# Quad 0 of a ReLU-squared attention: k split between a plain and a casting transfer, and turned ahead of q

## The chip, the cores and the metric

The kernel runs on one core of one Trainium2 chip. The metric is the device time of one execution in microseconds (us); lower is better. The engines are named as the profile names them: PE is TensorE's matmul, PEld its weight load, DVE is VectorE, ACT is ScalarE, POOL is GpSimd, SP is SyncE. SP, ACT and POOL can issue transfers (DMA); those that SP and ACT issue here are plain copies of float32, those of POOL cast float32 to bf16 on the way.

## The reference

Attention with a squared ReLU in place of softmax, and then a two-layer network with a leaky activation whose slope differs by column. Cut to what is computed:

```python
batch, n_heads, seq, head_dim = (8, 12, 448, 64)
n_tokens, d_model, d_ff = (3584, 768, 2048)

def _attn_ref(q, k, v):
    S = q.shape[2]
    scale = 1.0 / np.sqrt(q.shape[-1])
    scores = scale * np.matmul(q, k.transpose(0, 1, 3, 2))
    attn = np.maximum(scores, 0.0) ** 2 / S
    return np.matmul(attn, v)

def _moe_ref(x, w_in, w_out, alpha):
    h = x @ w_in
    g = np.maximum(h, 0.0) + alpha * np.minimum(h, 0.0)
    return g @ w_out
```

The heads of a token are put side by side between the two: `x` has 8 x 448 rows and 12 x 64 columns. All inputs and the output are float32.

## The kernel before

The attention is worked in 24 quads: quad `n` is four heads of one batch entry (three quads to an entry). A quad's q, k and v lie in tiles of 128 partitions x 2 x 7 x 64: two heads on the two halves of the partitions, two more in the second dimension, and the 448 rows of a head as 64 partitions x 7 blocks. Block `j` is thus 64 rows of each head.

For every quad, q and k have to be turned, so that the 64 features stand on the partitions: `T` is 128 x 2 x 7 x 128, with index 0 of its second dimension for q and 1 for k. Quads 0 to 5 are turned on TensorE (`turn_pe`): 14 transposes each for q and k into a PSUM bank, and a copy from there to `T`. Later quads are turned by a transposing transfer that SP issues (`turn_dma`, lines 159 to 166).

Then, for each of seven blocks `j`, `score_mm` (lines 171 to 180) makes the scores of k's block `j` against all of q with four matmuls in a pair of PSUM banks. It needs all seven blocks of q in `T` and one block of k. `relu` (line 182) takes the pair to a bf16 tile `rl`, on ScalarE ("A", line 185) or VectorE ("D", line 187) as a letter says; for the first quads the letters are `ADAAAAA`, so score 1 goes to VectorE. `square` (line 190) squares it into `at`, mostly on VectorE (line 195). `attnv` (line 198) multiplies all seven `at` tiles of a quad with v (line 205) and scales the result into `xT`. `sc` makes scores and relus of a list of blocks, `sq` the squares that are still owed.

The two layers follow: `f1` (lines 237 to 255) makes one of 16 slices of the hidden layer for one batch entry, six matmuls (line 239) and the activation on ScalarE and VectorE; `f2` (lines 257 to 270) makes the output of 128 rows by 384 columns from 16 matmuls (line 262) and sends it out.

All of this is one program in the order in which it is written; each engine runs its own instructions in that order, and waits between engines follow from the tiles that they share. PSUM's eight banks are handed out by hand: `take_pair` and `take_bank` give the pair or the bank that was taken longest ago, `hold` keeps one.

The start of the program is what the change touches. Lines 120 to 124: SP issues all of q of quad 0 as float32 (`qfirst`, 448 KB) and then alpha, ACT issues all of k (`kfirst`, 448 KB). GpSimd makes the identity matrix (line 125), then issues v of quad 0 (line 126), and q, k, v of quads 1 and 2 (lines 136 to 138), each as a casting transfer; the first half of `w_in` follows (lines 278 and 279). TensorE runs 36 matmuls of the identity with itself (lines 127 to 129). Lines 130 to 135 cast quad 0 to bf16: q's blocks 0 to 3 on VectorE and 4 to 6 on ScalarE, then k's blocks 0 and 1, and 2 to 6, on ScalarE. Line 280 turns quad 0, q first: each part of the copies goes into its own bank, and all four copies to `T` are VectorE's:

```python
    load_w_in(0)
    load_w_in(1)
    turn_pe(0, ((0, 4, "D"), (4, NJ, "D")), ((0, 2, "D"), (2, NJ, "D")))
    sc(ch(0, 0, 4))
    sq(3)
    load_qk(3)
    sc(ch(0, 4, 6))
    turn_pe(1)
    sc(ch(0, 6, 7))
    sq(4)
```

The next quads come in the same manner: quad 1 is turned after score 5 of quad 0, `attnv(0)` stands behind the first three scores of quad 1, quad 2 is turned behind score 3 of quad 1.

Of the kernel before, what the change touches and what calls it, by code (L numbers as in the profile page):

```python
# [10 lines left out]
F32 = mybir.dt.float32  # L11
BF16 = mybir.dt.bfloat16
# [4 lines left out]
NJ = 7  # L17
# [3 lines left out]
def kernel(  # L21
# [10 lines left out]
    nc = tc.nc  # L32
    B, H, S, D = q.shape
    d_model, d_ff = moe_w_in.shape
    assert H * D == d_model and S == PP * NJ and D == 64 and H % 4 == 0 and B % 2 == 0
    NG = H // 4
# [7 lines left out]
    singles = ctx.enter_context(tc.tile_pool(name="singles", bufs=1))  # L44
    raw_pool = ctx.enter_context(tc.tile_pool(name="raw", bufs=3))
    v_pool = ctx.enter_context(tc.tile_pool(name="v", bufs=7))
    perm_pool = ctx.enter_context(tc.tile_pool(name="perm", bufs=2))
    T_pool = ctx.enter_context(tc.tile_pool(name="T", bufs=4))
# [8 lines left out]
    ident = singles.tile([128, 128], BF16)  # L57
# [4 lines left out]
    psum = ps_pool.tile([128, 8, 512], F32)  # L62
# [5 lines left out]
    def take(lo, n):  # L68
        clock[0] += 1
        for i in range(lo, lo + n):  # L70
            taken[i] = clock[0]
# [12 lines left out]
    def take_bank():  # L84
        i = min(range(8), key=lambda i: (taken[i], i))
        take(i, 1)
        return psum[:, i]


    raw, vraw = {}, {}  # L90

    def load_qk(n):
        b, g = divmod(n, NG)
        for name, src in (("q", q), ("k", k)):
            t = raw_pool.tile([128, 2, NJ, D], BF16, tag=name, name=f"{name}raw")
            flat = src[b].rearrange("(m two) (pp j) d -> (two pp) m (j d)", two=2, j=NJ)
            nc.gpsimd.dma_start(out=t.rearrange("p m j d -> p m (j d)"), in_=flat[:, 2 * g:2 * g + 2])  # L97
            raw[(n, name)] = t

    def load_v(n):  # L100
        b, g = divmod(n, NG)
        t = v_pool.tile([128, 2, NJ, D], BF16, tag="v", name="vraw")
        flat = v[b].rearrange("(m two) (pp j) d -> (two pp) m (j d)", two=2, j=NJ)
        nc.gpsimd.dma_start(out=t.rearrange("p m j d -> p m (j d)"), in_=flat[:, 2 * g:2 * g + 2])  # L104
        vraw[n] = t
# [4 lines left out]
    def load_w_in(i):  # L110
        lo, hi = 512 * i, 512 * i + 512
        for hf in range(2):
            for e in range(2):
                nc.gpsimd.dma_start(out=w_in_sb[64 * hf:64 * hf + 64, :, e, lo:hi],  # L114
                                    in_=w_in_v[hf, e, :, :, lo:hi])
# [1 line left out]
    def load_w_out(h):  # L117
        nc.gpsimd.dma_start(out=w_out_sb[:, h], in_=w_out_v[h])

    first = {}  # L120
    for name, src, eng in (("q", q, nc.sync), ("k", k, nc.scalar)):
        first[name] = singles.tile([128, 2, NJ * D], F32, name=f"{name}first")
        eng.dma_start(out=first[name], in_=src[0].rearrange("(m two) (pp j) d -> (two pp) m (j d)", two=2, j=NJ)[:, :2])
    nc.sync.dma_start(out=alpha_sb, in_=moe_alpha.rearrange("(kf p) -> p kf", p=128))
    make_identity(nc, ident)
    load_v(0)
    warm = psum[:, 7, :128]
    for _ in range(36):
        nc.tensor.matmul(warm, ident, ident, start=True, stop=True)
    for name, cut in (("q", ((0, 4, nc.vector.tensor_copy), (4, NJ, nc.scalar.copy))),  # L130
                      ("k", ((0, 2, nc.scalar.copy), (2, NJ, nc.scalar.copy)))):
        t = raw_pool.tile([128, 2, NJ, D], BF16, tag=name, name=f"{name}raw")
        for lo, hi, copy in cut:
            copy(t[:, :, lo:hi].rearrange("p m j d -> p m (j d)"), first[name][:, :, D * lo:D * hi])  # L134
        raw[(0, name)] = t
    for n in range(1, NG):
        load_qk(n)
        load_v(n)


    T = {}

    def turn_pe(n, cuts=((0, NJ, "D"),), cuts_k=((0, NJ, "D"),)):
        t = T_pool.tile([128, 2, NJ, 128], BF16, tag="T", name="T")
        for i, name in enumerate("qk"):
            src = raw.pop((n, name))
            for lo, hi, eng in (cuts, cuts_k)[i]:
                ps = take_bank().bitcast(BF16)
                for j in range(lo, hi):
                    for s in range(2):  # L150
                        nc.tensor.transpose(ps[64 * s:64 * s + 64, 128 * j:128 * j + 128], src[:, s, j], ident)  # L151
                dst = t[:, i, lo:hi].rearrange("p j c -> p (j c)")
                if eng == "D":
                    nc.vector.tensor_copy(dst, ps[:, 128 * lo:128 * hi])  # L154
                else:
                    nc.scalar.copy(dst, ps[:, 128 * lo:128 * hi])
        T[n] = t

    def turn_dma(n):
        p = perm_pool.tile([128, 2, NJ, 2, D], BF16, tag="perm", name="perm")  # L160
# [10 lines left out]
    def score_mm(n, j):  # L171
        ps = take_pair()
        t = T[n]
        for r in range(2):
            for c in range(2):
                nc.tensor.matmul(ps[64 * c:64 * c + 64, r, :S],  # L176
                                 t[64 * r:64 * r + 64, 1, j, 64 * c:64 * c + 64],
                                 t[64 * r:64 * r + 64, 0, :, 64 * c:64 * c + 64],
                                 start=True, stop=True)
        return ps  # L180

    def relu(ps, eng):
        rl = rl_pool.tile([128, 2, S], BF16, tag="rl", name="rl")
        if eng == "A":
            nc.scalar.activation(rl, ps[:, :, :S], ACTF.Relu)  # L185
        else:
            nc.vector.tensor_scalar(rl, ps[:, :, :S], 0.0, None, ALU.max)  # L187
        return rl
# [31 lines left out]
    def sc(chunks):  # L220

        for n, j, eng in chunks:
            late.append((n, j, relu(score_mm(n, j), eng)))

    def sq(k=99, eng="D"):
        for g in late[:k]:
            square(*g, eng)
        del late[:k]
# [8 lines left out]
    def f1_mm(ps, b, ff, ks):  # L237
        for km in ks:
            nc.tensor.matmul(ps, w_in_sb[:, km // 2, km % 2, bass.ts(ff, 128)],  # L239
                             xT[b][:, km // 2, km % 2, :],  # L240
                             start=(km == 0), stop=(km == KM - 1))

    def f1_out(ps, b, ff):
        if b // 2 not in gT:
            gT[b // 2] = g_pool.tile([128, KF, 2 * S], BF16, tag="g", name="gT")
        neg = neg_pool.tile([128, S], F32, tag="neg", name="neg")
        nc.scalar.activation(neg, ps, ACTF.Relu, scale=-1.0)  # L247
        nc.vector.scalar_tensor_tensor(gT[b // 2][:, ff, (b % 2) * S:(b % 2) * S + S],  # L248
                                       neg, beta_sb[:, ff:ff + 1], ps, ALU.mult, ALU.add)
        sq(1)  # L250
# [24 lines left out]
    def ch(n, lo, hi, p=pat):  # L275
        return [(n, j, p[j]) for j in range(lo, hi)]

    load_w_in(0)
    load_w_in(1)
    turn_pe(0, ((0, 4, "D"), (4, NJ, "D")), ((0, 2, "D"), (2, NJ, "D")))  # L280
    sc(ch(0, 0, 4))
    sq(3)
    load_qk(3)
    sc(ch(0, 4, 6))
# [3 lines that stand above are left out]
# [5 lines left out]
    sq(2)  # L293
    sc(ch(1, 3, 4))
    turn_pe(2)
    sq(1)
    sc([(1, 4, "D"), (1, 5, "A"), (1, 6, "A")])
# [57 lines left out]
    f1s(0, 8, 9)  # L355
    ps = take_bank()[:, :S]
    f1_mm(ps, 0, 9, range(KM))
    turn_pe(4, ((0, NJ, "A"),))
    f1_out(ps, 0, 9)
    load_qk(7)  # L360
    load_v(7)
# [40 lines left out]
    for ff in range(4):  # L402
        ps = take_bank()[:, :S]
# [92 lines left out]
```

## Time and profile before

| what | value |
|---|---|
| time, median of 9 runs | 389.15 us (388.89 to 392.31) |
| the profiled execution's own time | 389.23 us |
| its span, first to last instruction | 387.5 us |
| PE busy | 378.6 us (98%), 3228 matmuls |
| DVE busy | 265.9 us (69%), 420 instructions |
| ACT busy | 206.5 us (53%), 332 instructions |
| POOL busy | 63.2 us (16%) |
| mean granted clock of TensorE | 0.998 |
| matmuls of line 239 | 768, 149.5 us |
| matmuls of line 262 | 912, 151.1 us |
| matmuls of line 176 (scores) | 672, 45.7 us |
| matmuls of line 205 (attention times v) | 672, 37.0 us |
| transfers, whole span | 43.06 MB, 111 GB/s |
| transfers, first 30 us | 5.72 MB, 191 GB/s |

The profile is of one execution. A busy PE need not be a PE at its peak, because matmuls are pipelined and their ends are modelled. Times in the views count from the start of the span; the 1.7 us between span and time lie outside of it. An instruction's row gives its start, the time that it (or a group of its like) takes, its engine, its line, and what it writes and reads; brackets give the idle time of the engine before it and what ended that.

### The profile page before, as it was taken

How to read it: one execution, taken by the hardware profiler on the slowest of the kernel's cores; microseconds unless marked ns; L12 is line 12 of the kernel's file. 1: busy time of each engine (PE TensorE's matmuls, PEld its weight loads, DVE VectorE, ACT ScalarE, POOL GpSimd, SP SyncE). 2: the span in 40 equal slices, each digit the busy share in tenths (PEclk: the TensorE clock that was granted, in tenths of full speed). 3: DMA queues.
4: the chain of work that ended last, by engine and by line, in shares of the span. 5: the costliest groups of instructions: out<-in, count | busy, mean ns of one | idle time of the engine just before them, and what ended most of it. 6: DMA issues, size and time to landing. Idle time of an engine off the chain costs nothing.

```text
span 387.5 us, 7916 instructions
## 1 busy us (share of the span) xinstructions
PE 378.6 (98%) x3228; PEld 211.9 (55%) x3228; DVE 265.9 (69%) x420; ACT 206.5 (53%) x332; POOL 63.2 (16%) x94
## 2 busy tenths in 40 slices
PE   8799999999999999999999999999999999999995
PEld 6444564555665456645555455654555545655564
DVE  3977876777868878789655896689754887626300
ACT  4977686355555664455445554547543475434311
POOL 7467211512022202022110221020000000000000
PEclk9999999999999999999999999999999999999999
DMA  9999999999493775787292871936024200120023
GB/s 181 186 204 205 203 213 214 147 164 201 102 156 69 117 131 73 130 139 114 46 176 51 136 120 42 179 57 133 22 63 108 70 0 23 42 61 2 20 71 75
DMA packets 71093, 43.06 MB, mean 111 GB/s; under 512 B 38160, under 2 KB 71056, under 8 KB 71056
## 3 DMA queue, kind: packets, MB, share of 16 engines
q0 software_dynamic: 26496, 22.35, 39.6%
q1 hardware_dynamic: 44128, 19.65, 24.3%
q10 hardware_dynamic: 432, 0.56, 0.4%
q8 instruction: 25, 0.41, 0.4%
q14 instruction: 12, 0.10, 0.1%
HBM read 45.62 MB, written 11.01 MB: 146 GB/s over the span
## 4 chain that ended last, share of the span: by engine, by line
PE 94%; ACT 1%; DVE 1%; DMA 1%; issue 0%; ACTq 0%
PE psum L239 38%; PE psum L262 38%; PE psum L176 9%; PE psum L205 8%; ACT rl L185 1%; PE psum L151 1%; DMA qfirst<-in_q_dram 1%; DVE at L195 1%; DVE T L154 0%; DVE rl L187 0%; ACT osb L264 0%; ACTq L270 0%; DVE qraw L134 0%; ACTq L264 0%; ACT xT L215 0%
## 5 line engine op out<-in xcount | busy, mean ns | idle before, releaser
L262 PE MATMUL psum<-w_out_sb,gT 128*128 128x384 bf16 (+2 forms) x912 | 151.1, 323 | 0.0
L239 PE MATMUL psum<-xT,w_in_sb 128*128 128x448 bf16 x768 | 149.5, 353 | 0.4 <-ACT rl L185 0.4
L262 PEld LDWEIGHTS <-gT 128*128 128x128 bf16 x912 | 86.7, 98 | 63.0 <-issue 8.2
L239 PEld LDWEIGHTS <-w_in_sb 128*128 128x128 bf16 x768 | 73.7, 98 | 72.4 <-issue 5.7
L248 DVE SCALAR_TENSOR_TENSOR gT<-neg,beta_sb,psum 128x448 bf16<-128x448 f32 x128 | 83.1, 676 | 30.7 <-ACT neg L247 30.7
L247 ACT ACTIVATE neg<-psum 128x448 f32<-128x448 f32 x128 | 69.3, 547 | 64.0 <-PE psum L239 60.2
L185 ACT ACTIVATE rl<-psum 128x896 bf16<-128x896 f32 x112 | 97.3, 935 | 1.1 <-PE psum L176 1.1
L195 DVE TENSOR_TENSOR at<-rl 128x896 bf16<-128x896 bf16 x162 | 90.7, 616 | 0.0
L187 DVE TENSOR_SCALAR rl<-psum 128x896 bf16<-128x896 f32 x56 | 60.8, 1086 | 41.0 <-PE psum L176 41.0
L264 ACT COPY osb<-psum 128x384 f32<-128x384 f32 (+2 forms) x57 | 27.0, 474 | 105.6 <-PE psum L262 96.6
L176 PE MATMUL psum<-T 64*64 64x448 bf16 x672 | 45.7, 356 | 2.5 <-DVE T L154 0.9
L97 POOL DMA_DIRECT2D qraw<-in_q_dram x23 | 16.5, 718 | 171.4 <-DVE perm L162 166.6
L205 PE MATMUL psum<-at,vraw 64*64 64x448 bf16 x672 | 37.0, 351 | 0.5 <-ACT rl L185 0.2
L205 PEld LDWEIGHTS <-vraw 64*64 64x64 bf16 x672 | 24.2, 106 | 10.8 <-issue 2.5
L176 PEld LDWEIGHTS <-T 64*64 64x64 bf16 x672 | 18.1, 105 | 21.6 <-issue 15.0
L216 DVE TENSOR_SCALAR xT<-psum 128x448 bf16<-128x448 f32 x23 | 14.4, 624 | 16.2 <-PE psum L205 11.8
L97 POOL DMA_DIRECT2D kraw<-in_k_dram x23 | 16.5, 717 | 14.9 <-PE psum L239 7.0
L104 POOL DMA_DIRECT2D vraw<-in_v_dram x24 | 17.3, 722 | 1.2 <-issue 0.6
L215 ACT ACTIVATE xT<-psum 128x448 bf16<-128x448 f32 x23 | 12.7, 553 | 3.0 <-PE psum L205 3.0
L162 DVE COPY perm<-qraw 128x896 bf16<-128x896 bf16 x18 | 11.0, 611 | 4.2 <-DMA T<-perm 2.6
L114 POOL DMA_DIRECT2D w_in_sb<-in_moe_w_in_dram x16 | 10.1, 629 | 8.1 <-DMA kraw<-in_k_dram 2.8
L162 DVE COPY perm<-kraw 128x896 bf16<-128x896 bf16 x18 | 10.9, 607 | 0.0
(22 smaller groups left out, 42.3 us busy)
## 6 DMA issues: line engine op xcount, KB each, us to landing
out_dram<-osb SPq DMA_DIRECT2D x110, 96.0 KB, 2.2
vraw<-in_v_dram POOLq DMA_DIRECT2D x24, 224.0 KB, 7.5
qraw<-in_q_dram POOLq DMA_DIRECT2D x23, 224.0 KB, 4.7
kraw<-in_k_dram POOLq DMA_DIRECT2D x23, 224.0 KB, 6.7
w_in_sb<-in_moe_w_in_dram POOLq DMA_DIRECT2D x16, 192.0 KB, 8.0
w_out_sb<-in_moe_w_out_dram POOLq DMA_DIRECT2D x2, 1536.0 KB, 18.5
kfirst<-in_k_dram ACTq DMA_DIRECT2D x1, 448.0 KB, 4.6
qfirst<-in_q_dram SPq DMA_DIRECT2D x1, 448.0 KB, 4.3
```

Source lines behind the costliest of these rows:

```text
L97: nc.gpsimd.dma_start(out=t.rearrange("p m j d -> p m (j d)"), in_=flat[:, 2 * g:2 * g + 2])
L162: nc.vector.tensor_copy(p[:, i], raw.pop((n, name)).rearrange("p s j d -> p j s d"))
L176: nc.tensor.matmul(ps[64 * c:64 * c + 64, r, :S], t[64 * r:64 * r + 64, 1, j, 64 * c:64 * c + 64], t[64 * r:64 * r + 64, 0, :, 64 * c:64 * ...
L185: nc.scalar.activation(rl, ps[:, :, :S], ACTF.Relu)
L187: nc.vector.tensor_scalar(rl, ps[:, :, :S], 0.0, None, ALU.max)
L195: nc.vector.tensor_tensor(a, rl, rl, ALU.mult)
L205: nc.tensor.matmul(ps[64 * s:64 * s + 64, r, :S], vv[64 * r:64 * r + 64, s, j, :], a[64 * r:64 * r + 64, s], start=(j == 0), stop=(j == NJ ...
L239: nc.tensor.matmul(ps, w_in_sb[:, km // 2, km % 2, bass.ts(ff, 128)], xT[b][:, km // 2, km % 2, :], start=(km == 0), stop=(km == KM - 1))
L247: nc.scalar.activation(neg, ps, ACTF.Relu, scale=-1.0)
L248: nc.vector.scalar_tensor_tensor(gT[b // 2][:, ff, (b % 2) * S:(b % 2) * S + S], neg, beta_sb[:, ff:ff + 1], ps, ALU.mult, ALU.add)
L262: nc.tensor.matmul(ps, gT[sb][:, ff, bass.ts(c, 128)], w_out_sb[:, hf, ff, lo:hi], start=(ff == 0), stop=(ff == KF - 1))
L264: nc.scalar.copy(o[:, lo:hi], ps)
```

## The change

Quad 0's k is split. Its first four blocks of seven (`FIRST = 4`) still come by ACT's plain transfer, now 256 KB, and are cast by ScalarE in one copy. The other three come as GpSimd's first casting transfer, straight into the bf16 tile. q still comes whole by SP's plain transfer; its two casts stay on VectorE and ScalarE, but ScalarE casts k's four blocks before q's last three.

GpSimd's order changes: the rest of k comes first, then q and k of quad 1, v of quad 0, q and k of quad 2, v of quad 1, v of quad 2 (before: v of quad 0, then q, k, v of quad 1, then q, k, v of quad 2).

The identity is multiplied 30 times instead of 36. `turn_pe` takes a list of parts, so that q and k can be turned piece by piece in any order. For quad 0 it turns k's blocks 0 to 3 first, with ScalarE's copy into `T`, then q's two parts with VectorE's copies; then come scores 0 to 2; then k's blocks 4 to 6 are turned, with VectorE's copy, and score 3 follows. Quad 4's call is written in the new form with the same engines as before (q's copy on ScalarE, k's on VectorE).

```diff
+    FIRST = 4
+    first, flat0 = {}, {}
+    for name, src, eng, hi in (("q", q, nc.sync, NJ), ("k", k, nc.scalar, FIRST)):
+        first[name] = singles.tile([128, 2, hi * D], F32, name=f"{name}first")
+        flat0[name] = src[0].rearrange("(m two) (pp j) d -> (two pp) m (j d)", two=2, j=NJ)[:, :2]
+        eng.dma_start(out=first[name], in_=flat0[name][:, :, :hi * D])
+        raw[(0, name)] = raw_pool.tile([128, 2, NJ, D], BF16, tag=name, name=f"{name}raw")
     nc.sync.dma_start(out=alpha_sb, in_=moe_alpha.rearrange("(kf p) -> p kf", p=128))
     make_identity(nc, ident)
+    nc.gpsimd.dma_start(out=raw[(0, "k")][:, :, FIRST:].rearrange("p m j d -> p m (j d)"),
+                        in_=flat0["k"][:, :, FIRST * D:])
+    warm = psum[:, 7, :128]
+    for _ in range(30):
+        nc.tensor.matmul(warm, ident, ident, start=True, stop=True)
+    for name, lo, hi, copy in (("k", 0, FIRST, nc.scalar.copy), ("q", 0, 4, nc.vector.tensor_copy),
+                               ("q", 4, NJ, nc.scalar.copy)):
+        copy(raw[(0, name)][:, :, lo:hi].rearrange("p m j d -> p m (j d)"), first[name][:, :, D * lo:D * hi])
+    load_qk(1)
     load_v(0)
-    warm = psum[:, 7, :128]
-    for _ in range(36):
-        nc.tensor.matmul(warm, ident, ident, start=True, stop=True)
-    for name, cut in (("q", ((0, 4, nc.vector.tensor_copy), (4, NJ, nc.scalar.copy))),
-                      ("k", ((0, 2, nc.scalar.copy), (2, NJ, nc.scalar.copy)))):
...
-    for n in range(1, NG):
-        load_qk(n)
-        load_v(n)
+    load_qk(2)
+    load_v(1)
+    load_v(2)
...
+    def turn_pe(n, parts=(("q", 0, NJ, "D"), ("k", 0, NJ, "D"))):
+        if n not in T:
+            T[n] = T_pool.tile([128, 2, NJ, 128], BF16, tag="T", name="T")
+        for name, lo, hi, eng in parts:
+            ps = take_bank().bitcast(BF16)
+            for j in range(lo, hi):
+                for s in range(2):
+                    nc.tensor.transpose(ps[64 * s:64 * s + 64, 128 * j:128 * j + 128], raw[(n, name)][:, s, j], ident)
+            dst = T[n][:, "qk".index(name), lo:hi].rearrange("p j c -> p (j c)")
+            copy = nc.vector.tensor_copy if eng == "D" else nc.scalar.copy
+            copy(dst, ps[:, 128 * lo:128 * hi])
...
-    turn_pe(0, ((0, 4, "D"), (4, NJ, "D")), ((0, 2, "D"), (2, NJ, "D")))
-    sc(ch(0, 0, 4))
+    turn_pe(0, (("k", 0, FIRST, "A"), ("q", 0, 4, "D"), ("q", 4, NJ, "D")))
+    sc(ch(0, 0, 3))
+    turn_pe(0, (("k", FIRST, NJ, "D"),))
+    sc(ch(0, 3, 4))
...
-    turn_pe(4, ((0, NJ, "A"),))
+    turn_pe(4, (("q", 0, NJ, "A"), ("k", 0, NJ, "D")))
```

More of the change, by code (lines that the diff above doesn't have):

```diff
@@ L118, in load_w_out @@
         nc.gpsimd.dma_start(out=w_out_sb[:, h], in_=w_out_v[h])
[L120 to L123, printed above, removed]
+    FIRST = 4
[5 more added lines that the diff above has]
+        raw[(0, name)] = raw_pool.tile([128, 2, NJ, D], BF16, tag=name, name=f"{name}raw")
@@ L124 @@
     nc.sync.dma_start(out=alpha_sb, in_=moe_alpha.rearrange("(kf p) -> p kf", p=128))
     make_identity(nc, ident)
-    load_v(0)
-    warm = psum[:, 7, :128]
-    for _ in range(36):
-        nc.tensor.matmul(warm, ident, ident, start=True, stop=True)
-    for name, cut in (("q", ((0, 4, nc.vector.tensor_copy), (4, NJ, nc.scalar.copy))),
-                      ("k", ((0, 2, nc.scalar.copy), (2, NJ, nc.scalar.copy)))):
[L132 to L135, printed above, removed]
@@ L136 @@
-    for n in range(1, NG):
-        load_qk(n)
-        load_v(n)
-    T = {}
[L143 to L157, printed above, removed]
+    nc.gpsimd.dma_start(out=raw[(0, "k")][:, :, FIRST:].rearrange("p m j d -> p m (j d)"),
+                        in_=flat0["k"][:, :, FIRST * D:])
```

## The prediction

> **What bounds the kernel now.** I read the busy time by stretch first, to find where anything but TensorE sets the pace (columns: stretch, length, then PE, PEld, DVE, ACT, POOL busy, clock, DMA share, GB/s).
>
> ```profile
> 7.60:14.80 7.20, 5.79 (x114) 3.43 (x112) 7.18 (x13) 7.20 (x10) 3.15 (x5) 1.00 1.22 190
> 14.80:19.70 4.90, 3.63 (x64) 1.83 (x61) 4.86 (x10) 4.90 (x8) 2.92 (x5) 1.00 1.18 185
> 19.70:22.00 2.30, 1.57 (x21) 0.71 (x20) 2.30 (x6) 2.30 (x5) 1.62 (x3) 1.00 1.23 205
> 22.00:30.00 8.00, 8.00 (x85) 4.35 (x85) 5.51 (x9) 4.80 (x8) 5.16 (x9) 1.00 1.25 203
> ```
>
> Until 22 us ScalarE and VectorE are both full while PE has gaps; from 22 us PE is full. So work added to ScalarE or VectorE before 22 us, or a later start of their packed stretch, delays the end by as much. Then the chain of waits over the first 30 us (start, us, what), for what starts that stretch:
>
> ```profile
> 0.74 4.25 DMA qfirst<-in_q_dram
> ...
> 5.02 0.44 DVE qraw L134
> ...
> 5.50 1.75 PE psum L151 x27
> ...
> 7.27 0.50 DVE T L154
> ...
> 7.82 0.60 PE psum L176 x8
> 8.42 0.60 ACT rl L185
> ```
>
> The landing of q, a cast, the transposes, a copy of T and the scores stand in a row. The timeline of 0 to 8 us (start, us, instruction) gives the durations:
>
> ```profile
> 1.36 4.02 PE L129 MATMUL psum<-ident 128*128 128x128 bf16 x36 [1.36 <-POOL ident masks.py:199]
> ...
> 5.50 0.96 PE L151 MATMUL psum<-ident,qraw 128*64 128x128 bf16 x14
> ...
> 6.18 0.89 DVE L154 COPY T<-psum 128x512 bf16<-128x512 bf16 x3 [0.74 <-PE psum L151]
> 6.25 0.98 PE L151 MATMUL psum<-ident,kraw 128*64 128x128 bf16 x14
> ...
> 7.16 1.04 PE L176 MATMUL psum<-T 64*64 64x448 bf16 x12
> 7.27 0.49 DVE L154 COPY T<-psum 128x640 bf16<-128x640 bf16 x1 [0.20 <-PE psum L151]
> ```
>
> VectorE's first relu starts at 7.79 and its first square at 8.79; ScalarE's first relu starts at 7.59 and lasts 0.92. Last, the DMA queues from 2.75 to 4.50 us (q10 carries k, q1 carries q):
>
> ```profile
> q10 hardware_dynamic: 187, 0.34, 50.4%
> q1 hardware_dynamic: 186, 0.33, 48.7%
> ```
>
> The two queues take turns packet by packet. In the microsecond before, q1 had sent 70 packets and q10 one, so q has a head start.
>
> **The change, part by part.**
>
> *Landings.* Before, q lands at 0.74+4.25 = 4.99 and k at 0.74+4.6 = 5.34. k's 256 packets shrink from 1792 to 1024 bytes. The stretch in which both take turns moves 186x(1792+1024) = 0.52 MB instead of 0.67 MB, at the window's 380 GB/s 0.37 us less; k's remaining 68 packets save 0.14 us more. So q lands at 4.62 and k at 4.83: k still last, although it now goes first. Bounds for k: 4.65 if the queues shared bytes rather than packets (2x262 KB at 380 GB/s from 2.75, and the 0.52 from data to landing), 5.34 if a packet cost the same whatever its size. I take packets by bytes, since 380 GB/s held at one packet size.
>
> *k's cast on ScalarE, ahead of q.* ScalarE's casts of 384 and 640 columns took 0.51 and 0.72, so 512 take 0.61: 4.86 to 5.47. PE starts transposing at 5.52 (a cast's end to PE's start was 0.05), where it started at 5.50. q's casts finish beside that: VectorE 0.43 from 4.65, ScalarE 0.51 from 5.47.
>
> *Transposes before the first score: 22 instead of 18.* 28 starts took 1.45 us (5.50 to 6.95), 0.054 each, with 0.31 for the last to end. The q blocks that VectorE copies first are now the 9th to 16th: ready at 5.52+15x0.054+0.31 = 6.64 (before 6.16). Its copies of 0.425 and 0.348 overlap by 0.08 and end at 7.35; the first score followed the copies by 0.09, so 7.44 instead of 7.16: **0.28 later**. The k copy that moves to ScalarE is ready at 6.21; by ScalarE's 0.91 for 896 columns and 0.55 for 448 it takes 0.55 to 0.6 and is done by 6.83, hidden under VectorE's q copies by 0.5; without that cover its excess would add whole.
>
> *k's last three blocks.* Their 0.35 copy stands behind the relu of score 1 on VectorE, inside the packed stretch; the 0.28+0.49 of k copies that it had before lay ahead of that stretch. Score 1 ends 0.61 after the first score's start (eight score matmuls took 0.57 at 7.82), so the relu starts at 8.05 instead of 7.79, its follower 1.00 later, and the squares another 0.27 after that: 9.32 instead of 8.79, **0.53 late**. Score 3 waits for that copy (end 9.40): its relu starts at 9.40+0.05+0.38 = 9.83 where three relus in a row put it at 7.59+2x0.92 = 9.43, 0.40 late. Queued behind the copy on VectorE are all squares and the T copies of quad 1; ScalarE gets 0.1 us of idle. What is late next is attnv(0) and then quad 2's transposes, both inside the packed stretch.
>
> *The casting transfer.* It stands where v of quad 0 stood, which was issued at 1.44 and landed 6.0 later, at 7.44. It moves 96 of 224 KB; the casting queue moved 0.40 MB from 5.25 to 7.5 us, 178 GB/s, so 128 KB less is 0.72 less: landing between 6.7 and 7.44. PE reaches these blocks after score 2, near 8.1, and VectorE wants them at 9.05; a landing after 8.7 would hold PE and every score behind it, one for one. The cover is 1.2 to 2 us; cost 0. The Trainium skill, "DMA: Bandwidth & Descriptors", Specifications, says that pieces under 512 bytes are written by read-modify-write, and these are 384; no row here shows one, and by it the landing would go toward the late end, still covered: the sum is the same.
>
> *Order on GpSimd's queue.* v(0) becomes fourth, where the fourth landed at 10.9 and its reader starts at 12.0; v(1) seventh (15.4, needed at 17.8); v(2) eighth (16.35, needed at 23.56). q and k of quad 1 move up by 0 to 0.72; those of quad 2 keep their places. w_in has 96 KB more ahead of it, 0.54 at most, against 1.3 of slack (its first four pieces land by 20.2, first read 21.46). Cost 0. Alpha's transfer stays behind q on its queue. Line 358's call for quad 4, rewritten, does what it did: 0.
>
> *30 warming matmuls instead of 36.* 36 took 4.02 us, 0.106 a start; 30 end at 4.74. Then PE idles 0.78 us until 5.52, where it idled 0.12, and again from about 6.9 to 7.44, where it transposed. The granted clock reads 1.00 in every stretch, yet the 14 transposes of q took 0.96 at 5.50 and 0.58 at 9.37, and weight loads of k 0.165 against 0.109: PE ran at half pace until about 7.16, 5.8 us after its first matmul. The bounds: paced by time since the first work, fast from 7.16, cost 0 (no gain: it isn't earlier); paced by unbroken work, fast from 5.52+5.8 = 11.3, or from 7.44+5.8 = 13.2. If PE is slow through score 3 only, scores take 0.37 each instead of 0.19: the relu of score 1 starts at 8.39, squares at 9.66, 0.87 late, and score 3's relu at about 10.36, 0.93 late.
>
> The Trainium skill, "TensorE: Matmul & The Clock Gate", Part 1, says that the clock is released by a sustained busy window of some 3.4 us that runs freely of the kernel. By it 30 matmuls (3.38 us) no longer fill one, and full pace would come between 8.9 and 14: 0.9 to 1.8 late in all, an estimate from that page; this trace's 5.8 us neither proves nor denies it.
>
> *Sum.* Against this execution's own 389.23 (span 387.5 and 1.7 around it, 0.08 above the median of 389.15): +0.53 with the pace as before, +0.93 with a pace late by some 3 us. I take the middle, +0.75: 389.23+0.75 = 389.98, say 390.0.
>
> **The rivals.**
>
> *The pace comes after 11 us: slower.* Quad 1's 28 transposes begin near 10.9; slow, their first copy starts at 11.72 (pace at 11.3: seven slow, seven fast, 0.22) to 11.97 (never fast), the k copy at 12.7 instead of 10.9. That is 1.3 to 1.8 late, **390.8**. For it: the 0.78 gap and the shorter warming. Against: PE still works most of the time from 1.36. It decides once pace comes later than about 11.0, where quad 1's copies pass 10.39+1.17.
>
> *k early, or the delay absorbed: no change.* With k at 4.65 all is 0.18 less; with quad 1's q and k landing earlier some of the wait at the T copies may go: **389.3**. Against: VectorE and ScalarE show no idle to absorb anything.
>
> *A late landing: slower.* k at 5.34 adds 0.51 to either sum (390.3 to 390.7), or the casting transfer lands past 8.7+0.7: **390.5**. For it: smaller packets. Against: the covers above.
>
> *A real gain: faster.* The first relus would have to start 1.2 us earlier, with k and q both down near 3.5: **387.9**. For it: 192 KB less ahead of the first cast. Against: the rate of the DMA queues allows 0.5.
>
> **How the numbers follow.** A measurement of this kernel can tell about 0.3% from no change, 1.17 us: slower is above 390.3, faster below 388.0. Forecast 0.41 (389.6 to 390.2, no change), late pace 0.36 (slower), absorbed 0.11 (no change), late landing 0.05 (slower), gain 0.07. So faster 0.07, same 0.52, slower 0.41. Range 389.0 to 391.2: from the absorbed case less a spread of 0.3 to the late pace with its 1.8 and 0.2.
>
> **What would show it.** Right: k lands after q, near 4.8; first score near 7.4; VectorE's k copy directly behind its first relu, squares from 9.3 on or later; the transposes of quad 1 show the pace (0.58 or 0.96 for 14). Wrong if k lands before 4.4, if score 3's relu starts before 9.4, or if PE after 22 us is no longer without gaps.

## The result, and the profile after

The changed kernel took 389.77 us (median of 25 executions, 388.90 to 390.61); the kernel before, over 76 executions, 389.06 (388.88 to 392.31). The ratio is 1.0017, with a 95% interval from 1.0011 to 1.0023: slower by a little, and inside the 0.3% that was called no change. The median moved by 0.71 us where 0.75 was forecast. The median hides how it came about: of the 25 times, 8 lie at 388.9 to 389.1, 8 at 389.5 to 390.1 and 9 at 390.4 to 390.6. The kernel before has 74 of its 76 times within 388.9 and 389.4.

The profiled execution of the changed kernel is one of the first group: 389.00 us, span 387.2. Its busy time by stretch, with the columns as before:

```profile
7.60:14.80 7.20, 5.67 (x114) 3.29 (x108) 7.06 (x13) 7.20 (x10) 3.45 (x6) 1.00 1.24 196
14.80:19.70 4.90, 3.73 (x72) 2.04 (x67) 4.79 (x9) 4.90 (x8) 3.15 (x5) 1.00 1.16 181
19.70:22.00 2.30, 1.67 (x25) 0.72 (x21) 2.30 (x6) 2.30 (x5) 1.45 (x3) 1.00 1.26 210
22.00:30.00 8.00, 8.00 (x85) 4.28 (x85) 5.58 (x10) 4.75 (x8) 5.22 (x8) 1.00 1.24 202
```

The shape is that of before: ScalarE is full up to 22 us, VectorE all but 0.14 and 0.11 us, PE full behind it. The timeline of the first 10 us:

```profile
1.36 3.38 PE L133 MATMUL psum<-ident 128*128 128x128 bf16 x30 [1.36 <-POOL ident masks.py:199]
...
4.77 0.61 DVE L136 CAST qraw<-qfirst 128x512 bf16<-128x512 f32 x1 [4.77 <-DMA qfirst<-in_q_dram]
5.03 0.62 ACT L136 CAST kraw<-kfirst 128x512 bf16<-128x512 f32 x1 [2.47 <-DMA kfirst<-in_k_dram]
...
5.70 0.41 PE L153 MATMUL psum<-ident,kraw 128*64 128x128 bf16 x8 [0.96 <-ACT kraw L136]
5.95 0.56 PE L153 MATMUL psum<-ident,qraw 128*64 128x128 bf16 x14
...
7.12 0.76 PE L175 MATMUL psum<-T 64*64 64x448 bf16 x12 [0.62 <-DVE T L156]
...
8.52 0.38 PE L175 MATMUL psum<-T 64*64 64x448 bf16 x4 [0.35 <-ACT rl L184]
8.75 0.34 DVE L156 COPY T<-psum 128x384 bf16<-128x384 bf16 x1
...
9.15 0.57 PE L175 MATMUL psum<-T 64*64 64x448 bf16 x8 [0.25 <-DVE T L156]
```

k lands at 5.00 (0.74 + 4.26), behind q at 4.77, and the order of the steps is the predicted one. But 14 transposes take 0.56 us already at 5.95, where the kernel before needed 0.96 at 5.50: in this execution PE had its full pace before its first transpose, and the first score stands at 7.12 in spite of 22 transposes ahead of it. The second profile of the same kernel, of an execution of 391.61 us, shows the other kind:

```profile
6.17 0.96 PE L153 MATMUL psum<-ident,qraw 128*64 128x128 bf16 x14
...
7.59 1.33 PE L175 MATMUL psum<-T 64*64 64x448 bf16 x12 [0.46 <-DVE T L156]
...
10.90 0.96 PE L153 MATMUL psum<-ident,qraw 128*64 128x128 bf16 x14
```

Here quad 0's and quad 1's transposes both run at half pace (0.96 for 14), and the first score comes at 7.59. No profile of the changed kernel fell into the middle group. The row to compare executions by is the first group of matmuls of line 239 (238 after the change) in the chain of waits: it marks where PE becomes full. It stands at 21.96 in the profile of before; in the two of the changed kernel (early pace first, late pace second, one line of the chain each):

```profile
21.92 1.67 PE psum L238 x8
```

```profile
23.49 1.67 PE psum L238 x8
```

### The profile page after: what moved, and what is told of

It reads as the page before. It is cut to its first block, busy times and chain, and to the rows that moved or that the text cites. A ratio compares the mean times of both kernels' runs of the same rounds, so it can differ in the third digit from the quotient of the medians.

```text
span 387.2 us, 7903 instructions
## 1 busy us (share of the span) xinstructions
PE 377.4 (97%) x3222; PEld 210.8 (54%) x3222; DVE 265.5 (69%) x419; ACT 206.7 (53%) x332; POOL 63.9 (17%) x95
## 4 chain that ended last, share of the span: by engine, by line
PE 94%; DVE 2%; DMA 1%; ACT 1%; issue 0%; ACTq 0%
PE psum L238 38%; PE psum L261 38%; PE psum L175 9%; PE psum L204 8%; DVE at L194 1%; DMA kfirst<-in_k_dram 1%; PE psum L153 1%; DVE T L156 1%; ACT rl L184 1%; DVE rl L186 1%; ACT osb L263 0%; ACT kraw L136 0%; ACTq L269 0%; ACTq L184 0%; ACTq L263 0%
```

## The experiments

All times are medians, each set beside executions of the kernel before on the same chip: 389.17 for the first four versions, 389.30 for the second four, 389.19 for the last three. A ratio here is not the quotient of the two medians and differs from it by up to 0.0008. Edits are against the changed kernel unless they say otherwise.

**The change again, for its spread.** No edit.

> The changed kernel once more, for its spread and a second profile. Pace theory (PE's full pace comes early in some executions and late in others): times again spread from 389.0 to 390.6 with groups, and the profile's time goes with the moment from which transposes run at full pace (14 in 0.58 us instead of 0.96): near 389.0 if before 7 us, 389.9 or more if after 9 us. Order theory (the moved copies and the transfers' landings make the spread): the profile's time goes with the landing of k and of the casting transfer, at the same pace of the transposes.

Six executions: 389.46, four from 390.57 to 390.70, and the profiled one, 391.61; ratio 1.0035 (1.0023 to 1.0047). k landed at 5.04, 0.04 from the first profile's, so its landing doesn't make the difference between the two profiles; the transposes' pace does. (391.61 is 1.0 above its own group; its PE was idle 0.56 us between 60 and 120 us, which the first profile was not. That part isn't explained.)

**36 and 40 warming matmuls.**

```diff
-    for _ in range(30):
+    for _ in range(36):
```

> The changed kernel with 36 warming matmuls as before; PE's idle time before its first transpose falls from 0.96 us to about 0.3. Pace theory: fewer late executions; median 389.0 to 389.4, spread under 1.2. Order theory: nothing changes, median 389.7, spread 389.0 to 390.5.

389.33, with 11 of 12 executions from 389.08 to 389.59 and one at 390.92, so the spread is 1.84 where under 1.2 was expected; ratio 1.0008 (0.9999 to 1.0016).

```diff
-    for _ in range(30):
+    for _ in range(40):
```

> The changed kernel with 40 warming matmuls, which last until about 5.7 us at half pace, so PE has no idle time before k's first transpose. Pace theory: the late executions are gone, all within 389.0 to 389.4, as tight as the kernel before. Order theory: median 389.7 and the wide spread stay.

389.22, all 11 executions from 389.08 to 389.73 (three above the 389.4 that was expected); ratio 0.9999 (0.9990 to 1.0008). With ten more matmuls on 128 columns, whose results nobody reads, no loss is left that these times can tell. In the profile all 40 take less time than the 36 of the kernel before (3.85 against 4.02), because full pace comes while they still run:

```profile
1.36 3.85 PE L133 MATMUL psum<-ident 128*128 128x128 bf16 x40 [1.36 <-POOL ident masks.py:199]
```

The moment differs from execution to execution: in the five profiles of versions with 40, the 40 took 3.85, 3.92, 4.13, 4.38 and 4.45 us. In the last of them (the version with the copy on ScalarE, below) quad 0's transposes still ran at half pace.

**The kernel before with 30.** Against the kernel before:

```diff
-    for _ in range(36):
+    for _ in range(30):
```

> The kernel before with 30 warming matmuls instead of 36 and nothing else; PE idles from 4.74 to 5.50 us. Pace theory: the spread of the changed kernel appears here too, median 389.3 to 390.2, slowest executions above 390. Order theory: as before, median 389.1, within 388.9 to 389.4.

389.65, from 389.15 to 391.19; ratio 1.0016 (1.0007 to 1.0025). The warming count alone, without any of the change's moves, costs what the change cost in its 25 executions (1.0017). Beside the same executions of the kernel before, though, the repeated change had 1.0035, so it isn't shown that the count alone makes the whole of the loss. The order theory fell with this run and with the 40. The profile shows a third kind, in which full pace comes between the scores of quad 0 (24 matmuls in 2.59) and the transposes of quad 1:

```profile
7.36 2.59 PE L176 MATMUL psum<-T 64*64 64x448 bf16 x24
...
9.88 0.58 PE L151 MATMUL psum<-ident,qraw 128*64 128x128 bf16 x14
```

**12 warming matmuls.**

```diff
-    for _ in range(30):
+    for _ in range(12):
```

> The changed kernel with 12 warming matmuls: they end near 2.8 us and PE idles for almost 3 us before its first transpose. Pace theory: an early full pace hardly ever happens; median 390.4 to 391.6, nothing below 389.4, quad 1's transposes at 0.96 for 14 in the profile. Order theory: 389.7 as with 30.

390.58, six executions from 390.14 to 390.64; ratio 1.0030 (1.0019 to 1.0041). This is the price of the late pace in full, 1.36 us above the version with 40 (1.2 by the two ratios).

**k by SP, q by ACT.**

```diff
-    for name, src, eng, hi in (("q", q, nc.sync, NJ), ("k", k, nc.scalar, FIRST)):
+    for name, src, eng, hi in (("k", k, nc.sync, FIRST), ("q", q, nc.scalar, NJ)):
```

> The changed kernel with its two plain transfers issued the other way round: k's 256 KB by SP, q by ACT; 30 warming matmuls. The sum's reading (q's queue had a head start of 70 packets, and k, cast first, landed last): k lands near 4.3 instead of 5.0, q near 4.9; PE's first transpose at 5.0, its idle time before it under 0.3, so the late executions become few too; first score at 6.7 to 6.9, median 388.7 to 389.0. Rival (the order of issue doesn't set the landing, or the start of the packed stretch doesn't set the end): k again near 5.0, or k early and the time 389.2 or more.

388.98, from 388.77 to 390.64, 5 of 12 above 389.3; ratio 1.0000 (0.9986 to 1.0014). k lands first, at 4.70 and not at 4.3, and q at 5.2; the first score comes at 6.92. The direction was right and the size of k's gain was overestimated by 0.4. PE idles 0.65 us before its first transpose, and late executions remain.

**k's rest copied ahead of the first relu.** Against the version with 40:

```diff
-    turn_pe(0, (("k", 0, FIRST, "A"), ("q", 0, 4, "D"), ("q", 4, NJ, "D")))
-    sc(ch(0, 0, 3))
-    turn_pe(0, (("k", FIRST, NJ, "D"),))
-    sc(ch(0, 3, 4))
+    turn_pe(0, (("k", 0, FIRST, "A"), ("q", 0, 4, "D"), ("q", 4, NJ, "D"), ("k", FIRST, NJ, "D")))
+    sc(ch(0, 0, 4))
```

> The 40-matmul version with k's last three blocks turned and copied ahead of score 0 and VectorE's first relu, as their counterparts were in the kernel before. If the copy behind the relu costs its 0.27 us at the end: 388.9 to 389.05. If the packed stretch absorbs it: 389.2, with the chain's entry into the full stretch of PE unmoved. A late casting transfer would hold score 0 now: then 389.5 or more.

389.16 (389.05 to 389.53); ratio 0.9993 (0.9982 to 1.0003). The interval is too wide to tell 0.27 us from nothing; the profiles decide it (PE is full 14.79 us behind the first score here and in the version with 40): VectorE's copy behind its relu cost nothing at the end.

**v of quad 0 ahead on GpSimd's queue.** Against the version with 40:

```diff
-    load_qk(1)
-    load_v(0)
-    load_qk(2)
-    load_v(1)
+    load_v(0)
+    load_qk(1)
+    load_v(1)
+    load_qk(2)
     load_v(2)
```

> The 40-matmul version with GpSimd's queue ordered as before behind the rest of k: v of quad 0 ahead of quad 1's q and k. If the reordering is free, as the sum has it: 389.2, within 0.15 of the 40-matmul version. If quad 1's earlier landing is worth something: 389.4 to 389.8, with PE waiting for q or k of quad 1.

389.18 (388.97 to 389.64); ratio 0.9999 (0.9991 to 1.0008): the queue's new order costs nothing that these times can tell.

**The swap with 36.** Both edits from above.

> The version with k's plain transfer by SP and q's by ACT, with 36 warming matmuls in place of 30: they last until 5.38 us, and PE's first transpose stood at 5.39. Pace theory: the late executions (5 of 12 above 389.3 with 30) go, all within 388.7 to 389.2, median 388.85, about 0.3 under the kernel before. If something else makes them late: the same spread up to 390.6.

388.92, all 11 executions from 388.72 to 389.19; ratio 0.9993 (0.9984 to 1.0002). It is the lowest median of all versions, 0.27 under the kernel before beside it, but its interval still holds 1.

**The same copy on ScalarE.** Against the version with 40:

```diff
-    turn_pe(0, (("k", FIRST, NJ, "D"),))
+    turn_pe(0, (("k", FIRST, NJ, "A"),))
```

> The 40-matmul version with the copy of k's last three blocks on ScalarE instead of VectorE, between its relus. If ScalarE's packed stretch sets when PE gets full (first score plus 14.79 us in every profile with an early pace): about 0.45 us later, first score plus 15.2, median 389.6. If VectorE's sets it, as the prediction had it: 0.2 to 0.27 earlier, 388.9 to 389.0.

389.72, 10 of 11 from 389.60 to 390.13; ratio 1.0017 (1.0009 to 1.0026). The copy takes ScalarE 0.49 us, and the median rises by 0.50:

```profile
9.80 0.49 ACT T L156
```

**The copy made twice on VectorE.** Against the version with 40, in `turn_pe` behind the copy:

```diff
             copy(dst, ps[:, 128 * lo:128 * hi])
+            if (n, name, lo) == (0, "k", FIRST):
+                copy(dst, ps[:, 128 * lo:128 * hi])
```

> The 40-matmul version with VectorE's copy of k's last three blocks made twice (the same values again), 0.27 us more on VectorE. If VectorE's stretch has slack against ScalarE's: first score plus 14.8 again, median 389.2 to 389.3. If VectorE sets the end: first score plus 15.05, 389.45 or more.

389.61 (389.44 to 390.54); ratio 1.0012 (1.0003 to 1.0021). Against the expectation from slack: PE is full 15.05 us behind the first score, as was expected if VectorE sets the end, and the median is 0.39 above the version with 40. The second copy in the chain, and the first matmuls of line 240 (238 before the two added lines):

```profile
9.20 0.36 DVE T L158
...
22.24 1.67 PE psum L240 x8
```

## Why the prediction was right, and where it was not

What the profiles have in common is best seen in a table, made from the timelines and chains (times in us; "idle" is PE's idle time ahead of its first transpose; "full" is where the chain's matmuls of line 239, 238 or 240 begin).

```
version                  time    idle  14 q transposes     first  full   full -
                                       quad 0   quad 1     score         score
before                   389.23  0.12  0.96     0.58       7.16   21.96  14.80
changed, first profile   389.00  0.96  0.56     0.58       7.12   21.92  14.80
changed, second profile  391.61  1.00  0.96     0.96       7.59   23.49  15.90
12 warming matmuls       390.57  2.91  0.95     0.96       7.58   23.50  15.92
before with 30           389.65  0.93  0.96     0.58       7.36   22.37  15.01
36 warming matmuls       389.25  0.38  0.56     0.58       7.36   22.15  14.79
40 warming matmuls       389.38  0.89  0.56     0.58       7.53   22.32  14.79
40, k's rest ahead       389.12  0.00  0.56     0.58       7.14   21.93  14.79
40, v first              389.16  0.31  0.56     0.58       7.23   22.02  14.79
swap, 30                 388.85  0.65  0.58     0.58       6.92   21.71  14.79
swap, 36                 388.78  0.20  0.58     0.58       6.87   21.66  14.79
40, copy on ScalarE      390.13  0.00  0.95     0.58       7.75   22.93  15.18
40, copy twice           389.44  0.49  0.56     0.58       7.19   22.24  15.05
```

In every row but the second profile's, the time is "full" plus 367.1 to 367.3; so what the start does is passed on whole, as the prediction's first reading had it. And with an early pace PE is full 14.79 or 14.80 us behind the first score, whether the change is in or not. Only three things move that difference: a pace that stays slow into the scores or quad 1, work added to ScalarE, and VectorE's second copy.

*Landings: right in order, off in size.* k came last, at 5.00 instead of 4.83, and q at 4.77 instead of 4.62. The term that was off is the rate. From 2.75 to 4.10 us the queues still took turns (169 and 166 packets), but moved 349 GB/s where the sum held 380:

```profile
DMA packets 335, 0.47 MB, mean 349 GB/s; under 512 B 0, under 2 KB 335, under 8 KB 335
## 3 DMA queue, kind: packets, MB, share of 16 engines
q1 hardware_dynamic: 166, 0.30, 56.9%
q10 hardware_dynamic: 169, 0.17, 38.1%
```

Not all of that is the size of the packets. The first 0.2 us are slow in both profiles (197 GB/s before, 123 after) and weigh more in the shorter stretch; from 2.95 to 4.10 us the rates are 407 before and 388 after, 5% apart. The landing also varies: in the nine profiles that send k in this way it lies from 5.00 to 5.41.

*Cast and transposes: right for the late pace.* The cast of k took 0.62 (0.61 said). From PE's start to the first score the sum had 1.92 at half pace; the second profile shows 1.85 (5.74 to 7.59). At full pace it is 1.42 (5.70 to 7.12). So the 0.28 for the first score is 0.43 in the one kind of execution and -0.04 in the other: the prediction held half pace through all of quad 0's transposes in both of its sums, and did not think of a full pace that comes earlier than before, which two of the four profiles with 30 warming matmuls show.

*k's last three blocks: wrong.* Two steps failed. Score 3 was said to wait for their copy; it reads block 3, which is among the first four. The profile shows it at 8.52, released by ScalarE's relu, ahead of the copy's end; score 4, at 9.15, is what waits, and ScalarE comes to it later. So score 3's relu starts near 9.2, before the 9.4 that was named as a sign of being wrong.

And the 0.27 on VectorE did not pass on to the end. It did pass on as far as quad 2's transposes, as the prediction had it: they start 7.16 us behind the first score before and 7.41 after. But the relu that PE's full stretch waits for starts at the same time. The chain before:

```profile
14.32 0.53 PE psum L151 x14
...
20.80 1.12 ACT rl L185
...
21.96 1.67 PE psum L239 x8
```

And after:

```profile
14.53 0.53 PE psum L153 x14
...
20.81 1.06 ACT rl L184
...
21.92 1.67 PE psum L238 x8
```

ScalarE is the engine that sets the end: from its first relu (7.59 before, 7.55 after) to the end of the one that PE waits for (21.91 and 21.87) it works without a gap, 14.32 us both times. VectorE was as good as full (14.34 of 14.40 us before), but what stood on it had room against ScalarE. The two last experiments measure the room. The copy on ScalarE, 0.49, moves PE's full stretch by 0.39 and the time by 0.50. A second copy on VectorE, 0.38 with its wait, moves it by 0.26 (the median by 0.39; what makes the rest of that is open). So VectorE had room for the first copy and about 0.1 us more.

*Casting transfer, GpSimd's order: right.* The rest of k landed at 6.44 (1.44 + 5.0), ahead even of the early bound of 6.7; nothing waited for it. The order of v made no difference that the times can tell (389.18 and 389.22).

*The pace of PE: the mechanism was a rival, and it makes the loss.* The first bound (paced by the time since the first work, so always from 7.16) fell: pace differs from execution to execution of one kernel. The rival gave 390.8 for a late pace; the version with 12 and the late group give 390.4 to 390.6. The forecast's value lay between its two sums, 0.53 and 0.93, and the measured median lies there too, but as the middle of a mixture: early executions 0.05 below the kernel before, late ones 1.4 above it. The forecast had 0.27 of its 0.75 from the copy that costs nothing at the end, and neither sum describes a group that was measured. So the number was right, and that 0.71 met 0.75 is luck; of its reasons the pace held, the later first score held in the late executions, and the copy did not.

That the number of warming matmuls decides how often the pace is late is shown from both sides. Above 390 us lie 15 of the 31 executions of the changed kernel with 30, 1 of 12 with 36, and 2 of 55 of all versions with 40 (both in the last two experiments); 3 of 12 with the swap and 30, none of 11 with the swap and 36; of the kernel before, 6 of 162 with its 36 and 3 of 11 with 30. Whether it is the idle time ahead of the transposes or the number itself was not separated: each edit changed both, and in single profiles the idle time doesn't decide (full pace at the first transpose with 0.96 and 0.89 us of idle time, half pace with 0.00 and 0.12). The Trainium skill, "TensorE: Matmul & The Clock Gate", Part 1, has a reason that fits: a busy window of about 3.4 us that runs freely, so that its place against the kernel differs by execution. No run here shows the window itself. Thirty matmuls last 3.38 us, and two profiles with 30 show full pace from the first transpose on, two do not; how much idle time such a window bears was not measured.

## What to carry to other kernels

When a change moves the first real matmul, count the warming matmuls again: they should last until that matmul in the slowest case. Here 40, which ended at 5.81 at the latest, with the first transpose at 5.90, held nothing up (40 against 30: 0.55 us in the median, and a spread of 0.65 instead of 1.7). A median between groups of times is no price of any step; look at the single times first, and take profiles of more than one group. Before a step inside a packed stretch is priced in full, ask which of the packed engines the end waits for, and which block of data the waiting instruction really reads.

## What the runs showed of the hardware that had not been expected

VectorE's cast of q's first four blocks (512 columns, float32 to bf16) took 0.49 to 0.61 us in the seven profiles where it began between 4.77 and 4.92, and ended at 5.38 to 5.41 in all seven, the earliest start with the longest cast; where it began at 5.00 or later (six profiles) it took 0.43. Something held VectorE until about 5.0 us. GpSimd was issuing casting transfers then (one from 4.41 to 5.13), but it went on issuing them (the next from 5.12 to 5.84) beside the casts that took 0.43, and no run took them away, so the cause is open.
